# Reordered slots of an attention kernel beside its MLP: the norm's power behind the visit, stores and kept factors issued later

## The chip, the cores and the metric

The kernel runs on one core of a Trainium2 chip. The metric is the device time of one execution in microseconds (us); before the change the median of three runs is 1456.99 us. All data are float32. The engines are TensorE (PE, its weight loads are PEld), VectorE (DVE), ScalarE (ACT), GpSimd (POOL) and SyncE (SP), whose queue issues nearly all DMAs.

## The reference, cut to what matters

```python
def rmsnorm(x, g):
    rms = np.sqrt(np.mean(x * x, axis=-1, keepdims=True) + 1e-06)
    return x / rms * g
q_n, k_n = rmsnorm(q, g_q), rmsnorm(k, g_k)          # batch 8, heads 12, seq 448, head_dim 64
scores = np.matmul(q_n, k_n.transpose(0, 1, 3, 2)) / np.sqrt(64)
attn = np.exp(scores - scores.max(-1, keepdims=True))
attn = attn / (attn.sum(-1, keepdims=True) + 1e-09)
x = np.matmul(attn, v).transpose(0, 2, 1, 3).reshape(3584, 768)
h = x @ w_in                                         # 768 x 2048
out = (h - np.tanh(h)) @ w_out                       # 2048 x 768
```

## The kernel before, in words

Attention goes in 48 steps, one for each pair of heads of each batch (six to a batch). `slot(s)` does the values of step s and the scores of step s + 1, prepares the q and k of later steps, and lets the MLP of an earlier batch run between its pieces. The MLP is a generator (`mlp`): each `yield` tells the time of the matmul just written, and `run(ns)` draws matmuls until that much time is spent. Every engine works through its own queue in the order in which instructions are written, so the order of `slot`, `run` and the MLP is the order of all queues. There is no scheduler behind it.

**The visit.** `visit(s, av)` is PE's stretch of attention: scores of the last, short key chunk of step s + 1 (L552, exp into `p_last`), then values of step s in alternation with scores of chunks 0 and 1 (L618 and L552), the short chunk of values (L606), `divide`, and the scores of chunk 2. The score banks are three (`banks["sc"][:3]`), so the second wave of chunk 0 waits until the exp of `p_last` has emptied a bank. `divide` copies the values' sum (ACT L735), adds the other half (DVE L736) and multiplies by the reciprocal of the softmax sum (DVE L740, two).

**Between two visits** a slot has 14 points, with a fifteenth of its MLP time ahead of each and behind the last. In the kernel before they are, for steps in the block layout: scale q and k of step s + 2 by their norm (`scale_blocks`, L516); transpose q; transpose k (`turn_blocks`, L526, L530, then ACT L531) and load q/k of step s + 4 (`load_blocks`, L483, eight DMAs); the first addition of the softmax sum (L583) and the square of step s + 3 (ACT L487); the third chunk (L589); the norm's row sums (`norm_blocks`, L494); the short chunk (L596, two) and the exchange of the norm's halves (`meet_blocks`, ACT L501, four); transpose the softmax sum (`fold`, L693); its row sums (`fold_rest`, L700); half of `gather` (ACT L708, four) and `power_blocks`; the other half; `spread_sums` (DVE L716, L717, ACT L719); nothing; `turn_sums` (L725). `power_blocks` adds the halves (DVE L506), turns them into a mean (DVE L507) and has GpSimd raise it to the power -0.5 (POOL L509). The q/k tiles of step s + 4 take the place that step s + 2 leaves when L516 has read it (`qk_nat`, two buffers).

**The MLP.** Both layers are one level of Strassen's scheme with seven products in the order 1, 5, 6, 2, 3, 7, 4 (`ORDER`). A hidden layer (`hidden`, L804) has four groups of seven products; per group, a tanh on ACT and a subtraction that makes g (L850: product 2's on DVE, those of 3, 7 and 4 on POOL, written behind the product that follows, from `late["todo"]`). The tanh tile `th` has two buffers, and so have the others of `part`. Batch 0 is projected plainly (`project_first`, L1190), batch 1 by `project`; from batch 2 on two batches share a projection with two levels (`project_pair`, L1029), whose inner sums are POOL's (L1003, tile `u`, four buffers), apart from the four of its first outer product, which DVE makes at its start. Beside batch 1, `inner_steps` makes the inner factors of w_out on POOL (L955), one step a product, and keeps them in DRAM (`keep`, L937, five DMAs a factor), in a room that later holds `g2`.

**Weights** come through a ring of six slots (`ring_load`, L412 to L420): a product loads for the one four products later. Output tiles are transposed on DVE (L910) and stored with four DMAs (`store`, L913). Everything stands in SP's one queue: ring loads, q/k loads, v loads, kept factors, stores. In a slot beside a hidden layer its order is two v tiles, two ring loads, the eight q/k loads, five ring loads.

**Which MLP lies beside which slot** (`gap_ns`): slots 12 to 19 share batch 1's hidden layer, its projection and the first product of batch 2 evenly, 15.96 us each by the kernel's own count. Then, for each pair of batches, eight slots beside two hidden layers (15.7 us each) and four beside the projection (28.7 us each). The last pair has only four slots left.

## Time and profile before

| | |
|---|---|
| median of three runs | 1456.99 us (1453.01 to 1460.95) |
| the profiled execution | 1456.48 us, span 1454.7 us |
| mean granted clock of TensorE | 0.983 |
| busy: PE, DVE, POOL, ACT | 93%, 70%, 47%, 38% of the span |
| POOL's power, L509 | 33 times, 4843 ns each |
| POOL's inner sums, L1003 | 2217 to 2552 ns each |
| POOL's subtraction, L850 | 96 times, about 1.2 us each |
| w_f from w_in, w_inner, w_out | 4.0, 4.0, 4.6 us from issue to landing |
| slots 12 to 19 | 278.7 to 479.4 us |
| slots beside the hidden layers of two pairs | 479.4 to 674.9 and 826.0 to 1021.8 us |
| slots beside the first two `project_pair` | 674.9 to 826.0 and 1021.8 to 1173.1 us |
| slots 44 and 45 | 1173.1 to 1220.8 us |

How to read it: a slot is counted from the start of one visit (the L552 matmuls on 224 columns) to the start of the next. In the lists of waits a line is "engine line <- what ended the wait: total us, times, longest us". A line of the chain or of a timeline is "start us, duration us, engine, line, what". The windows give, for each stretch, the length, the busy time of PE, PEld, DVE, ACT and POOL with numbers of instructions, the granted clock, the DMA engines' busy share and GB/s. "issue" in the chain is time in which the engine waited for nothing that the profile shows; the long duration of a power on POOL appears in it.

### The profile page before, as it was taken

How to read it: one execution, taken by the hardware profiler on the slowest of the kernel's cores; microseconds unless marked ns; L12 is line 12 of the kernel's file. 1: busy time of each engine (PE TensorE's matmuls, PEld its weight loads, DVE VectorE, ACT ScalarE, POOL GpSimd, SP SyncE). 2: the span in 40 equal slices, each digit the busy share in tenths (PEclk: the TensorE clock that was granted, in tenths of full speed). 3: DMA queues.
4: the chain of work that ended last, by engine and by line, in shares of the span. 5: the costliest groups of instructions: out<-in, count | busy, mean ns of one | idle time of the engine just before them, and what ended most of it. 6: DMA issues, size and time to landing. Idle time of an engine off the chain costs nothing.

```text
span 1454.7 us, 29095 instructions
## 1 busy us (share of the span) xinstructions
PE 1352.1 (93%) x11336; PEld 1050.3 (72%) x11336; DVE 1012.3 (70%) x1471; ACT 552.9 (38%) x1326; POOL 685.2 (47%) x397
## 2 busy tenths in 40 slices
PE   7989899998799998999999999999989989999995
PEld 3468744576688787777766787878767678998884
DVE  5999898577786675668887775757988756323743
ACT  7856564334334444444222244453423233211000
POOL 4756474167653426243555534442645631423561
PEclk9999999999999999999999999999999999999998
DMA  7879787889787745464464764545536473555554
GB/s 171 193 200 293 229 233 197 233 256 309 261 230 229 185 115 175 105 184 113 128 161 113 180 193 114 144 144 136 170 103 173 116 192 110 163 174 156 147 144 99
DMA packets 371687, 253.53 MB, mean 174 GB/s; under 512 B 282196, under 2 KB 310228, under 8 KB 371540
## 3 DMA queue, kind: packets, MB, share of 16 engines
q1 hardware_dynamic: 371536, 251.57, 62.4%
q8 instruction: 92, 1.51, 0.4%
q14 instruction: 55, 0.45, 0.1%
q10 hardware_dynamic: 4, 0.00, 0.0%
HBM read 205.23 MB, written 46.27 MB: 173 GB/s over the span
## 4 chain that ended last, share of the span: by engine, by line
PE 36%; DVE 12%; issue 4%; POOL 1%; ACT 1%; DMA 1%; SPq 1%; DVEq 0%; POOLq 0%
PE mm L1029 17%; PE mm L804 12%; PE sc L552 4%; PE sc L618 2%; DVE rows L596 1%; DVE acc L1036 1%; DVE rows L589 1%; DVE rows L583 1%; DVE rr_mine L494 1%; DMA out_dram<-th 1%; DVE qk_n L516 1%; POOL rr_mine L509 1%; DVE qk_n L693 1%; DVE xT_more L740 1%; DVE s L1036 1%
## 5 line engine op out<-in xcount | busy, mean ns | idle before, releaser
L509 POOL TENSOR_TENSOR rr_mine<-rr_mine,neg_half 128x28 f32<-128x28 f32 x33 | 159.8, 4843 | 342.2 <-ACT sum_g L708 215.1
L552 PE MATMUL sc<-qT,kT 64*32 64x448 f32 (+1 forms) x3072 | 231.3, 513 | 37.1 <-ACT p_last L558 36.0
L804 PE MATMUL mm<-xT,w_f 128*128 128x224 f32 x1104 | 221.4, 354 | 9.3 <-DVE s L1036 4.1
L804 PE MATMUL mm<-tt,w_f 128*128 128x224 f32 x1044 | 211.7, 357 | 11.0 <-DMA w_f<-w_in 7.8
L804 PEld LDWEIGHTS mm<-xT,w_f 128*128 128x128 f32 x1104 | 207.4, 190 | 17.0 <-DVE s L1036 4.8
L804 PEld LDWEIGHTS mm<-tt,w_f 128*128 128x128 f32 x1044 | 197.3, 192 | 27.0 <-issue 13.6
L552 PEld LDWEIGHTS sc<-qT,kT 64*32 64x32 f32 x3072 | 76.9, 109 | 117.5 <-ACT p_last L558 52.8
L1029 PE MATMUL mm<-u,w_f 128*128 128x224 f32 x672 | 136.8, 354 | 8.9 <-issue 7.7
L1029 PEld LDWEIGHTS mm<-u,w_f 128*128 128x128 f32 x672 | 126.1, 190 | 13.9 <-issue 13.9
L618 PE MATMUL sc<-p,v_nat 64*32 64x448 f32 x1120 | 133.4, 566 | 0.0
L1029 PE MATMUL mm<-gT,w_f 128*128 128x224 f32 (+1 forms) x480 | 132.2, 429 | 0.7 <-DVE s L1036 0.7
L736 DVE TENSOR_TENSOR xT<-xT,sc 128x448 f32<-128x448 f32 x26 | 16.1, 621 | 163.4 <-PE sc L552 83.7
L1029 PEld LDWEIGHTS mm<-gT,w_f 128*128 128x128 f32 x480 | 90.4, 190 | 39.4 <-issue 37.1
L708 ACT COPY sum_g<-sum 32x14 f32<-32x14 f32 x280 | 56.3, 201 | 137.1 <-DVE sum L700 103.4
L1029 PE MATMUL mm<-g,w_f 128*128 128x224 f32 (+1 forms) x360 | 100.6, 434 | 4.7 <-DVE s L1036 4.7
L1029 PEld LDWEIGHTS mm<-g,w_f 128*128 128x128 f32 x360 | 68.4, 192 | 35.4 <-issue 29.1
L850 POOL TENSOR_TENSOR gT<-s,th 128x448 f32<-128x448 f32 x60 | 71.7, 1210 | 46.9 <-ACT th L849 44.7
L558 ACT ACTIVATE p<-sc 128x448 f32<-128x448 f32 x132 | 71.9, 545 | 45.9 <-PE sc L552 37.2
L849 ACT ACTIVATE th<-s 128x448 f32<-128x448 f32 x96 | 54.9, 575 | 68.2 <-POOL gT L850 21.4
L1190 PE MATMUL mm<-gT,w_out 128*128 128x448 f32 x192 | 74.6, 543 | 0.2 <-POOL w_out L90 0.2
L531 ACT ACTIVATE kT<-kT,g_col 128x448 f32<-128x448 f32 x33 | 22.1, 669 | 136.6 <-DVE kT L530 136.6
L1003 POOL TENSOR_TENSOR u<-g 128x896 f32<-128x896 f32 x18 | 39.9, 2217 | 68.0 <-PE mm L1029 40.8
(188 smaller groups left out, 2505.1 us busy)
## 6 DMA issues: line engine op xcount, KB each, us to landing
w_f<-w_in SPq DMA_DIRECT2D x196, 384.0 KB, 4.0
w_f<-w_inner SPq DMA_DIRECT2D x63, 512.0 KB, 4.0
w_f<-w_out SPq DMA_DIRECT2D x42, 512.0 KB, 4.6
w_raw<-in_moe_w_out_dram SPq DMA_DIRECT2D x16, 768.0 KB, 5.2
out_dram<-th SPq DMA_DIRECT2D x192, 56.0 KB, 2.0
w_in<-w_out SPq DMA_DIRECT2D x21, 384.0 KB, 5.2
qk_nat<-in_q_dram SPq DMA_DIRECT2D x132, 56.0 KB, 2.2
qk_nat<-in_k_dram SPq DMA_DIRECT2D x132, 56.0 KB, 2.3
```

The costliest lines, as they stand in the source:

```text
L509: nc.gpsimd.tensor_tensor(out=mine, in0=mine, in1=neg_half[:, :1].to_broadcast([P, 2 * NJ]), op=ALU.pow)
L552: nc.tensor.matmul(tiles[h][i * BL : (i + 1) * BL, :n], lhsT=kT[r, c * P + at : c * P + at + BL], rhs=qT[r, first : first + n], start=True ...
L558: nc.scalar.activation(p[:, h, c if c < 2 else 0, :], tiles[h][:, :n], AF.Exp, scale=1.0 if rr is None else rr[:, 0, 2 * c + h : 2 * c + h ...
L618: nc.tensor.matmul(av[g][i * BL : (i + 1) * BL, :S], lhsT=v_nat[keys, h, c, m * BL : (m + 1) * BL], rhs=p[keys, h], start=first, stop=True ...
L708: nc.scalar.copy(out=acc[h * BL : (h + 1) * BL, g], in_=part[g * BL : (g + 1) * BL, h * NJ : (h + 1) * NJ])
L804: nc.tensor.matmul(bank[:, f * HS : (f + 1) * HS], lhsT=w[:, c * width + f, :], rhs=moving[p](c), start=(first and f == 0 and c == 0), sto ...
L849: nc.scalar.activation(th, h, AF.Tanh, bias=0.0, scale=1.0)
L850: eng.tensor_tensor(out=g[:, rows, cols], in0=h, in1=th, op=ALU.subtract)
L1003: eng.tensor_tensor(out=u, in0=a, in1=z, op=ALU.subtract)
L1029: nc.tensor.matmul(bank[:, :n], lhsT=w(i), rhs=mv, start=(first and i == 0), stop=(i == len(moving) - 1), skip_group_check=not first,)
L1036: nc.vector.tensor_tensor(out=out, in0=x, in1=y, op=ALU.add)
L1190: nc.tensor.matmul(bank[:, :S], lhsT=w_out_row(f, n // HC)[:, n % HC * P : (n % HC + 1) * P], rhs=g[:, f, :], start=(f == 0), stop=(f == C ...
```

## The change

The power becomes a function of its own, and the slot's points are written in another order. The mean is finished late in the slot (`meet_rest`); the power itself is written directly behind the next visit, ahead of the first point. The additions of the softmax sum come first; scaling and transposing q and k follow, and `load_blocks` is written with the scaling. Squares, norm and exchange come behind `fold_rest`. `spread_sums` copies on DVE where it copied on ACT. Slots 12 to 14 lie beside the hidden layer of batch 1 (20.9 us of MLP each), slots 15 to 19 beside its projection and what is ahead (13.0 us each). A store's DMAs are written one product later, behind the next ring load (two steps later for batches 0 and 1); `step_out` counts. The kept inner factors are written one step later, in another order, and the next outer factor is fetched one step later. The four first inner sums of `project_pair` are now made on POOL during the odd batch's hidden layer, behind product 6 of each group (`first_inner`).

```diff
--- before.py
+++ after.py
@@ -500,12 +500,16 @@
         for g in range(P // BL):
             nc.scalar.copy(out=other[g * BL : (g + 1) * BL], in_=mine[(g ^ 1) * BL : ((g ^ 1) + 1) * BL])
 
-    def power_blocks(s):
+    def meet_rest(s):
 
         mine, other = normed["rr", s]
         nc.vector.tensor_tensor(out=mine, in0=mine, in1=other, op=ALU.add)
         nc.vector.tensor_scalar(out=mine, in0=mine, scalar1=1.0 / D, scalar2=1e-6, op0=ALU.mult, op1=ALU.add)
         normed["rr", s] = mine
+
+    def power_blocks(s):
+
+        mine = normed["rr", s]
         nc.gpsimd.tensor_tensor(
             out=mine, in0=mine, in1=neg_half[:, :1].to_broadcast([P, 2 * NJ]), op=ALU.pow
         )
@@ -716,7 +720,7 @@
         nc.vector.reduce_sum(total, acc.rearrange("p g j -> p j g"), axis=AX.X)
         nc.vector.reciprocal(total, total)
         wide = whole[s] = late["blocks"].tile([2 * BL, NJ, BL], F32, name="sum_w")
-        nc.scalar.copy(out=wide, in_=total[:, :, None].to_broadcast([2 * BL, NJ, BL]))
+        nc.vector.tensor_copy(out=wide, in_=total[:, :, None].to_broadcast([2 * BL, NJ, BL]))
 
     def turn_sums(s):
 
@@ -798,6 +802,7 @@
                 w = built(j, p).rearrange("p f (n d) -> p (f n) d", d=P)
             else:
                 ring_load(ring_steps.index((b, layer, j, p)) + 5)
+                step_out()
                 w = ring_tiles[b, layer, j, p].rearrange("p (n d) -> p n d", d=P)
             for f in range(width):
                 for c in range(depth):
@@ -863,6 +868,8 @@
 
             def use(p, bank):
                 v = view(bank)
+                if b > PAIRED and b % 2 and p == 6:
+                    first_inner(b - 1, j)
                 if j == SETS - 1 and p in ahead:
                     x_sums(b + 1, range(HC), ahead[p], nc.gpsimd)
                 if p == 1:
@@ -908,12 +915,22 @@
 
         o = part("th").rearrange("p f s -> p (f s)")
         nc.vector.transpose(out=o, in_=y if b >= FIRST else y.rearrange("r (c p) -> r p c", c=NCH))
-        for i in range(P // BL):
-            d = n * P + i * BL
-            nc.sync.dma_start(
-                out=out[b * S : (b + 1) * S, d : d + BL].rearrange("(j t) d -> t j d", t=BL),
-                in_=o[i * BL : (i + 1) * BL].rearrange("t (j d) -> t j d", d=BL),
-            )
+
+        def issue():
+            for i in range(P // BL):
+                d = n * P + i * BL
+                nc.sync.dma_start(
+                    out=out[b * S : (b + 1) * S, d : d + BL].rearrange("(j t) d -> t j d", t=BL),
+                    in_=o[i * BL : (i + 1) * BL].rearrange("t (j d) -> t j d", d=BL),
+                )
+
+        late["out"].append([1 if b >= PAIRED else 2, issue])
+
+    def step_out(by=1):
+        for entry in late["out"]:
+            entry[0] -= by
+        while late["out"] and late["out"][0][0] <= 0:
+            late["out"].pop(0)[1]()
 
     def calm_step(twice=False):
         for _ in range(1 + twice):
@@ -953,12 +970,13 @@
             )
             for n, (out, x, y, op) in enumerate(work):
                 yield lambda: nc.gpsimd.tensor_tensor(out=out, in0=x, in1=y, op=op)
-                if n == 0 and i + 1 < len(OUTER):
+                if n == 1 and i + 1 < len(OUTER):
                     fetch_outer(i + 1)
+            yield lambda: None
+            keep(i, 1, block(sums, 0, 2))
+            keep(i, 4, block(sums, 2, 2))
             keep(i, 0, a11)
-            keep(i, 1, block(sums, 0, 2))
             keep(i, 3, a12)
-            keep(i, 4, block(sums, 2, 2))
             keep(i, 6, a22)
             yield lambda: None
 
@@ -970,6 +988,15 @@
             else:
                 fn()
 
+    def first_inner(b, i):
+
+        g, us = late["g", b], late.setdefault("us", {})
+        KB = HF // 2
+        x11, x12, x21, x22 = (g[:, f : f + KB, cols] for f in (0, KB) for cols in (slice(0, HS), slice(HS, S)))
+        u = us[1, i] = late["pair"].tile([P, KB, HS], F32, name="u", bufs=4)
+        a, z = ((x12, x11), (x22, us.get((1, 0))), (x22, x12), (x21, us.get((1, 1))))[i]
+        nc.gpsimd.tensor_tensor(out=u, in0=a, in1=z, op=ALU.subtract)
+
     def project_pair(b):
 
         g = [late.pop(("g", b)), late.pop(("g", b + 1))]
@@ -977,7 +1004,7 @@
         KB = HF // 2
         HOME = {1: (0, 0), 5: (0, 0), 3: (1, 1), 6: (1, 1), 2: (0, 1), 4: (0, 1), 7: (1, 0)}
         acc, acc2 = (late["pair"].tile([P, HC, S], F32, name=name) for name in ("acc", "acc2"))
-        us = {}
+        us = late.pop("us")
 
         def rows(p, f, n, cols):
             which, half = HOME[p]
@@ -1011,9 +1038,6 @@
         }
         inner_plan = {5: 0, 6: 1, 7: 2, 4: 3}
         inner_at = {6: 0, 3: 1, 7: 2, 4: 3}
-        for i in range(4):
-            inner_sum(OUTER[0], i, V)
-
         def at(k, q):
 
             p = OUTER[k]
@@ -1078,6 +1102,7 @@
         for k, p in enumerate(OUTER):
             step = ring_steps.index((b, 2, p, 0))
             ring_load(step + 5)
+            step_out()
             w = ring_tiles[b, 2, p, 0].rearrange("p (f d) -> p f d", d=P)
             bank = mm_bank()
             q = 0
@@ -1093,6 +1118,7 @@
             banks = {}
             for i, q in enumerate(ORDER):
                 ring_load(step + 6 + i // 2)
+                step_out()
                 w = ring_tiles[b, 2, p, 1 + i // 2][:, i % 2 * HB : (i % 2 + 1) * HB].rearrange("p (f d) -> p f d", d=P)
                 first = q not in (2, 3, 7)
                 bank = banks[q] = mm_bank() if first else banks[{2: 1, 3: 5, 7: 6}[q]]
@@ -1172,6 +1198,8 @@
             n = (k + HC) % CD
             if f == 0:
                 bank = mm_bank()
+            if f == CF // 2:
+                step_out(2)
             if k < HC:
                 weight(CF + HF + HF * (m + 1) // (HC * CF))
             elif m < HC * CF + 2:
@@ -1203,7 +1231,7 @@
         late["inner"] = inner_steps()
 
     def mlp():
-        late["todo"], late["keep"], late["inner"], late["calm"] = [], [], None, []
+        late["todo"], late["keep"], late["inner"], late["calm"], late["out"] = [], [], None, [], []
         for b in range(PAIRED):
             yield from hidden(b)
             yield from project(b) if b else project_first(b)
@@ -1222,6 +1250,8 @@
             fn()
         while late["calm"]:
             calm_step()
+            step_out()
+        step_out(2)
 
     stream = mlp()
     spent = [0.0, 0.0]
@@ -1244,8 +1274,10 @@
 
         if s < 2 * NP:
             return H_NS / 12 if s % NP < 3 else 4 * S / ENGINE_NS * CD * CF / 12
+        if s < 2 * NP + 3:
+            return H_NS / 12
         if s < 2 * NP + 8:
-            return (H_NS + O_NS + AHEAD_NS) / 32
+            return (O_NS + AHEAD_NS) / 20
         return (H_NS if (s - 2 * NP - 8) % 12 < 8 else PAIR_NS) / 16
 
     def has(s):
@@ -1339,30 +1371,25 @@
         folded = following and s + 1 >= FOLDED
         first = s + 3 == TURNED
 
-        def scale_or_turn():
-            if first:
-                turn(s + 2, sc_bank(), sc_bank())
-            else:
-                scale_blocks(s + 2)
-
+        scaled = rows and not first
+        normed_now = ahead and not first
+        if scaled:
+            power_blocks(s + 2)
         work = (
-            ((rows, scale_or_turn),),
-            ((rows and not first, lambda: turn_blocks(s + 2, 0)), (first, lambda: load_blocks(s + 3))),
-            ((rows and not first, lambda: turn_blocks(s + 2, 1)), (has(s + 4), lambda: load_blocks(s + 4))),
-            ((following, lambda: add(s + 1, False)), (ahead and not first, lambda: square_blocks(s + 3))),
-            ((following, lambda: add_third(s + 1)),),
-            ((ahead and not first, lambda: norm_blocks(s + 3)),),
-            ((following, lambda: add_last(s + 1)), (ahead and not first, lambda: meet_blocks(s + 3))),
+            ((following, lambda: add(s + 1, False)), (first, lambda: turn(s + 2, sc_bank(), sc_bank()))),
+            ((following, lambda: add_third(s + 1)), (first, lambda: load_blocks(s + 3))),
+            ((following, lambda: add_last(s + 1)),),
+            ((scaled, lambda: scale_blocks(s + 2)), (has(s + 4), lambda: load_blocks(s + 4))),
+            ((scaled, lambda: turn_blocks(s + 2, 0)),),
+            ((scaled, lambda: turn_blocks(s + 2, 1)),),
             ((folded, lambda: fold(s + 1)),),
-            ((folded, lambda: fold_rest(s + 1)), (first, lambda: square_blocks(s + 3))),
-            (
-                (folded, lambda: gather(s + 1, 0)), (ahead and not first, lambda: power_blocks(s + 3)),
-                (first, lambda: norm_blocks(s + 3)),
-            ),
-            ((folded, lambda: gather(s + 1, 1)), (first, lambda: meet_blocks(s + 3))),
-            ((folded, lambda: spread_sums(s + 1)), (first, lambda: power_blocks(s + 3))),
+            ((folded, lambda: fold_rest(s + 1)), (ahead, lambda: square_blocks(s + 3))),
+            ((folded, lambda: gather(s + 1, 0)),),
+            ((ahead, lambda: norm_blocks(s + 3)), (folded, lambda: gather(s + 1, 1))),
+            ((ahead, lambda: meet_blocks(s + 3)), (folded, lambda: spread_sums(s + 1))),
             (),
-            ((folded, lambda: turn_sums(s + 1)),),
+            ((folded, lambda: turn_sums(s + 1)), (ahead, lambda: meet_rest(s + 3))),
+            (),
         )
         for point in work:
             run(4 * gap / (len(work) + 1))
```

## The prediction

> **What bounds the kernel now.** I read the page, the waits of TensorE (PE), the chain in order of time, the timelines of single engines, then SP's waits. PE is busy 93% of the span, so only what makes it wait or run slower counts.
>
> The waits of PE (total, times, longest) name ScalarE's exp of the last key chunk. The windows below them show an unstalled slot, a stalled one, and a stretch at half clock:
>
> ```profile
> PE sc L552 <- ACT p_last L558: 36.0, 18, 4.9
> PE mm L804 <- DMA w_f<-w_in: 7.8, 2, 5.8
> ```
>
> And the windows (us of the window; busy us and instructions of PE, PEld, DVE, ACT, POOL; granted clock; DMA):
>
> ```profile
> 479.40:500.90 21.50, 21.50 (x213) 18.17 (x212) 14.71 (x25) 9.80 (x26) 7.31 (x5) 1.00 0.87 225
> 526.80:551.10 24.30, 22.50 (x216) 18.95 (x215) 15.52 (x26) 11.15 (x30) 8.10 (x5) 1.00 0.50 142
> 506.60:510.00 3.40, 3.40 (x56) 2.18 (x47) 0.00 (x0) 1.63 (x3) 0.00 (x0) 0.50 0.00 0
> ```
>
> A slot (one visit of attention, then a quarter of a hidden layer) takes 21.5 us unstalled, about 24.25 us stalled: 2.75 us lost in each of 15 slots (7 beside each of the first two pairs of batches, one beside the third). Each of four stretches like the last line costs a further 1.7 us there. Who causes the stall is in the chain:
>
> ```profile
> 648.04 1.10 POOL rr_mine L509
> 649.14 3.65 issue
> 652.79 1.14 POOL g L850
> ...
> 653.95 0.58 ACT th L849
> 654.52 0.42 ACT s L869
> 654.94 0.27 ACT p_last L558
> ...
> 655.25 0.56 PE sc L552
> ```
>
> GpSimd's power (L509) starts 2.6 us before the visit of 650.63 and runs 4.78 us. The subtraction at L850 queues behind it, a tanh needs the buffer that L850 frees, and `p_last` stands behind that tanh on ScalarE. PE waits until 655.25.
>
> The wait that is hidden today is on SP: first its longest wait of all, then its timeline and PE's in the slot that ends with this visit:
>
> ```profile
> SPq L483 <- DVE qk_n L516: 246.7, 26, 15.9
> ```
>
> ```profile
> 637.82 1.90 SPq L483 DMA_DIRECT2D qk_nat<-in_q_dram  x4
> 639.76 2.04 SPq L483 DMA_DIRECT2D qk_nat<-in_k_dram  x4
> 641.90 4.61 SPq L412 DMA_DIRECT2D w_f<-w_in  x5
> ```
>
> ```profile
> 648.27 2.43 PE L804 MATMUL mm<-xT,w_f 128*128 128x224 f32 x12
> ```
>
> SP stands at the q/k loads until `scale_blocks` (L516) ends; five ring loads queue behind. The first holds the weights of product 1, the last before the next visit. It is issued at 641.90, takes 3.7 us to land (the view of `w_f`; the five reach 4.9), and PE wants it at 648.27: 2.7 us to spare.
>
> **What the Trainium skill says.** *DMA: Bandwidth & Descriptors*, "Anatomy of one DMA — SWDGE (gpsimd) path": a DMA's semaphore wait happens on the issuing sequencer. The SP lines agree: 246.7 us of waiting, with later loads behind. *SBUF — State Buffer*, "SBUF: two separate sides": a VectorE instruction with two SBUF inputs and a GpSimd one exclude each other, each for its whole length. It agrees for GpSimd's subtractions: L583 takes 1.08 us alone and 2.76 beside one (687.76). It does not for the power: L996 takes 1.08 us inside one (704.37). *TensorE: Matmul & The Clock Gate*, "Part 1: The HAM clock gate (the "warmup" mystery)": after idling, the clock is halved for about 3.4 us. The 0.50 line agrees. No page prices the power; the trace does.
>
> **The change, part by part.** Times are after V, the start of L736 behind a visit (634.68 here); PE wants product 1 at V+13.6.
>
> *Power behind the visit.* POOL's queue becomes subtraction, power, subtraction. The power's input comes from `meet_rest`, last on VectorE before the visit. So it runs about V-3.5 to V+1.3, in the visit, where POOL has nothing else to do. `p_last` then waits only for VectorE: laid out with the trace's durations it starts 1.8 us earlier than today, leaving some 0.9 us of the 2.75. By itself: 15 x 1.85 = 28 us gained, up to 41 with the whole stall, plus up to 5 x 1.7 of half clock.
>
> *Order of the slot.* `add`, `add_third` and `add_last` now precede the scaling. L516 ended at V+3.1. From the starts of the trace: L736 0.65, two L740 1.34, L583 1.18, L871 0.53, L589 1.01, two L596 1.30, L873 0.54, L516 1.09, sum V+7.6. The loads at L483 keep their place in SP's order: two ring loads, eight q/k loads, five ring loads. So the eight start at V+7.7 and take 4.1 us, the load for product 1 goes out at V+11.8 and lands at V+15.5. PE waits 1.9 to 2.0 us in every slot that has q/k loads. Bounds: 1.0 if the rest of the order saves VectorE a microsecond, 3.2 with the slowest landing. ScalarE catches up in that time, so the two stalls don't add; the new one replaces the old: 7.6 (L516) + 4.2 (q/k) + 3.7 (landing) + 2.4 (product) + 5.5 (unstalled visit with its restart) + 0.1 = about 23.5, say 23.6 us a slot, against 24.25.
>
> *First inner sums on POOL.* Four subtractions of 1.07 to 2.04 us leave VectorE at the head of `project_pair`, where PE has no idle time today: nothing gained. In the odd batch's hidden layer POOL gets one of 2.2 us (L1003: 2239 ns) per slot. Nothing holds it back, so it starts when the power ends, V+1.3, amid L740, L583 and L589, all with two SBUF inputs: one of them waits about 2.2 us. L516, SP and product 1 follow: 25.8 us for the slots of odd batches. Bounds: 0 if it falls between them, 2.2.
>
> Sum for the two stretches beside hidden layers (479.4 to 674.9, 826.0 to 1021.8; 391.3 us now): 8 x 23.6 + 8 x 25.8 = 395.2, plus half clock after idle stretches of 2 to 4 us, taken at six (four today, four to ten possible): 10.2. That is 405.4, or 14 more. Beside the third pair nothing is left to load, so there the stall and its half clock go: -4.6.
>
> *3 and 5 slots in batch 1* (278.7 to 479.4, 200.7 us). The MLP share is 20.9 and 13.0 us instead of 15.96. Four slots beside the hidden layer lose about 22 us today, 11 of them before a `w_f` load that came late behind q/k loads and kept factors (PE mm L804, 5.8, then half clock). In the three new ones POOL runs its sums of 1.27 us straight after the power, against VectorE's adds: L516 at V+11 to 12, ring loads behind the q/k loads 4 to 7 us late in two slots, with half clock about 17 in all. In the five short ones VectorE's 16 us of work and ScalarE's copies for the norm (`meet_blocks`, now close to the visit) run some 3.5 us into it, so `p_last` is late by about 2 each: 10, where 1 is lost now. Together +4; bounds -15 and +12.
>
> *Stores and kept factors later.* The stores stand behind one ring load more; the five kept DMAs a step later no longer wait for POOL (1 to 4 us a time). Worth up to -5 (in the span of batch 1, inside its bounds); a store's `th` buffer comes free at most one product later. Zero, covered by the other `th` buffer; without it L910 waits, as 18.2 us in all do now.
>
> *The spread copy on VectorE.* 0.56 us off ScalarE (L719), on VectorE 0.25 to 0.65; no row shows it, I take 0.5, ahead of nothing that PE waits for. Zero.
>
> *Slots beside `project_pair`* (302.4 us, some 27 lost to VectorE and the bank): the adds move ahead of PE's bank copies, four sums leave. Zero, bounds -8 and +8.
>
> **Sum:** 14 - 4.6 + 4 = 13.5. The profiled execution took 1456.5 (span 1454.7 and 1.8 around it; the median of the runs is 1457.0), so 1470.
>
> **Rivals.** (1) Faster: the load is not what ends the wait, because SP gets to it in time. It decides below about V+9.7 for the issue. Then even slots take 22.4 and odd ones 24 (0.9 us and 2.2 us of port left): 371 instead of 391, -5 in the third pair, -12 in batch 1, since the late `w_f` there goes too: 1419. For it: stalls named by the page are all ScalarE's and POOL's; against it: SP's queue order and eight issues of half a microsecond. (2) Nothing in the sum: the inner sum meets no VectorE instruction, batch 1 breaks even, and the adds ahead of the bank copies cost 8 beside `project_pair`. Then 16 x 23.6 + 7 = 385 (-6), -4.6 and +8: about 1454. For it: the port is only held 2.2 us a slot; against it: three of VectorE's four first instructions need it. (3) Slower still: every stall of an odd slot brings half clock and `project_pair` takes its upper bound: 1486.
>
> **Numbers.** Forecast (1462 to 1482) 0.43; rival 1 (1405 to 1445) 0.30; rival 2 (1446 to 1464) 0.15; rival 3 (1482 to 1495) 0.12. The range must reach into rival 1: 1418 to 1487. Half a per cent, 7 us, is about what a measurement can tell from no change: faster 0.31, same 0.16, slower 0.53. The likeliest case alone: 1462 to 1482.
>
> **What would show it.** Right: PE sc L552 <- ACT p_last near zero, and in its place waits of product 1 (L804) for DMA w_f<-w_in, some 2 us, 16 times; SP's wait at L483 ending about V+7.7; slots of 23.6 and 25.8 us, VectorE's longer where POOL subtracts behind the power. Wrong: unstalled slots of 21.5 to 22 us (rival 1), `p_last` still late in them, or the loss sitting in batch 1 or `project_pair`.

## The result and the profile after

The changed kernel takes 1456.66 us (median of 12 runs, 1451.67 to 1458.57), the kernel before in the same measurement 1460.43 us (1453.01 to 1462.06). The ratio is 0.9977, 95% interval 0.9963 to 0.9991: 3.4 us faster, inside the half per cent, where 1470 had been forecast. The profiled execution took 1454.87 us, span 1453.1, against 1454.7 before, so the two traces are compared stage by stage. First what PE waits for in the changed kernel:

```profile
PE mm L809 <- DMA w_f<-w_in: 22.1, 10, 5.2
PE mm L809 <- DVE s L884: 10.6, 5, 2.3
PE sc L556 <- ACT p_last L562: 10.2, 6, 5.2
```

The wait for `p_last`, 36.0 us in 18 cases before, is down to 10.2 us, none of it beside a hidden layer of batches 2 to 5. In its place stands `w_f`, 7.8 us before. The second line is the same wait under another name: a matmul that waits for several semaphores is put down to the one that came last by the profile, and run 7 below, which moves only loads, removes both lines.

Then the windows of six stages: slots 12 to 19, the hidden layers of the first pair, its `project_pair`, the same two of the second pair, slots 44 and 45. Of the kernel before:

```profile
278.67:479.41 200.74, 184.45 (x1726) 151.95 (x1725) 147.66 (x204) 84.23 (x227) 112.12 (x65) 0.98 0.82 248
479.41:674.87 195.46, 182.02 (x1692) 151.17 (x1691) 124.01 (x200) 87.78 (x230) 73.71 (x45) 0.98 0.55 152
674.87:826.00 151.13, 142.72 (x1024) 105.60 (x1023) 122.64 (x164) 41.85 (x115) 91.12 (x44) 0.99 0.53 135
826.00:1021.82 195.82, 182.27 (x1692) 151.16 (x1691) 126.21 (x206) 87.69 (x230) 69.03 (x41) 0.98 0.55 152
1021.82:1173.13 151.31, 141.30 (x1023) 104.95 (x1022) 122.71 (x165) 41.72 (x115) 90.70 (x44) 1.00 0.54 136
1173.13:1220.82 47.69, 45.57 (x425) 37.68 (x424) 31.28 (x52) 20.10 (x52) 9.19 (x5) 0.96 0.56 160
```

And of the changed kernel:

```profile
277.93:469.04 191.11, 182.83 (x1726) 152.92 (x1725) 141.59 (x204) 78.47 (x210) 108.28 (x67) 0.99 0.83 255
469.04:669.88 200.84, 181.61 (x1691) 147.92 (x1690) 150.35 (x215) 86.83 (x233) 82.29 (x47) 0.97 0.52 148
669.88:821.48 151.60, 143.29 (x1024) 107.08 (x1023) 119.53 (x169) 38.62 (x109) 88.01 (x43) 0.98 0.54 140
821.48:1021.20 199.72, 179.15 (x1691) 145.09 (x1690) 148.29 (x209) 85.26 (x223) 80.48 (x47) 0.98 0.51 147
1021.20:1174.71 153.51, 143.98 (x1023) 107.83 (x1022) 119.22 (x167) 38.63 (x109) 88.32 (x42) 0.98 0.54 138
1174.71:1219.73 45.02, 44.19 (x426) 37.03 (x425) 32.58 (x50) 18.98 (x50) 10.81 (x6) 1.00 0.59 165
```

The first number behind the two ends of a window is the stage's length: -9.6 in batch 1, +9.3 in the two hidden stretches together, +2.7 beside the paired projections, -2.7 in slots 44 and 45; the rest of the span gives -1.3. The forecast had +4, +14, 0 and -4.6. So two large movements cancel, and the one with the wrong sign is batch 1.

The hidden stretches move as forecast, by less. SP, POOL, VectorE and PE in one odd-batch slot of the changed kernel (V, the start of L740, which was L736 before, is 623.79 here):

```profile
633.26 1.90 SPq L483 DMA_DIRECT2D qk_nat<-in_q_dram  x4
635.20 2.04 SPq L483 DMA_DIRECT2D qk_nat<-in_k_dram  x4
637.34 2.32 SPq L412 DMA_DIRECT2D w_f<-w_in  x5
```

```profile
620.28 4.78 POOL L513 TENSOR_TENSOR rr_mine<-rr_mine,neg_half 128x28 f32<-128x28 f32 x1
625.03 2.08 POOL L998 TENSOR_TENSOR u<-gT 128x896 f32<-128x896 f32 x1
```

```profile
623.79 0.62 DVE L740 TENSOR_TENSOR xT<-xT,sc 128x448 f32<-128x448 f32 x1 [3.60 <-ACT xT L739]
624.45 3.13 DVE L744 TENSOR_TENSOR xT<-xT,rs_T 64x448 f32<-64x448 f32 x2
627.61 1.09 DVE L587 TENSOR_TENSOR rows<-p 128x896 f32<-128x896 f32 x1
628.62 0.62 DVE L878 TENSOR_TENSOR s<-mm,s 128x448 f32<-128x448 f32 x1
629.16 1.08 DVE L593 TENSOR_TENSOR rows<-rows,p_full 128x896 f32<-128x896 f32 x1
630.27 1.27 DVE L600 TENSOR_TENSOR rows<-rows,p_last 64x448 f32<-64x448 f32 x2
631.57 0.62 DVE L880 TENSOR_TENSOR s<-mm,s 128x448 f32<-128x448 f32 x1
632.12 1.08 DVE L520 TENSOR_TENSOR qk_n<-qk_nat,rr_mine 128x896 f32<-128x896 f32 x1
```

```profile
636.25 2.54 PE L809 MATMUL mm<-tt,w_f 128*128 128x224 f32 x12 [0.99 <-DVE g L855]
640.81 0.43 PE L809 MATMUL mm<-xT,w_f 128*128 128x224 f32 x1 [2.02 <-DMA w_f<-w_in]
```

The power now ends inside the visit. The scaling (L520) ends at V+9.4, because `u` runs across the two multiplications by the reciprocal at L744: 3.13 us for the pair, where run 4, without `u`, shows 1.27. The q/k loads start 0.06 us after the scaling, the ring load for product 1 goes out at V+13.6, and PE stands still for 2.02 us until it lands.

### The profile page after: what moved, and what is told of

Its sections match the earlier page's. It is cut to its first block, busy times and chain, and to the rows that moved or that the text cites. A ratio compares the mean times of both kernels' runs of the same rounds, so it can differ in the third digit from the quotient of the medians.

```text
span 1453.1 us, 29070 instructions
## 1 busy us (share of the span) xinstructions
PE 1348.9 (93%) x11336; PEld 1045.7 (72%) x11336; DVE 1044.5 (72%) x1494; ACT 535.4 (37%) x1291; POOL 705.5 (49%) x409
## 3 DMA queue, kind: packets, MB, share of 16 engines
q8 instruction: 92, 1.51, 0.4%
## 5 line engine op out<-in xcount | busy, mean ns | idle before, releaser
L809 PE MATMUL mm<-xT,w_f 128*128 128x224 f32 x1104 | 231.0, 365 | 36.3 <-DMA w_f<-w_in 16.9
L809 PEld LDWEIGHTS mm<-xT,w_f 128*128 128x128 f32 x1104 | 214.1, 196 | 47.1 <-DVE s L884 19.8
L556 PE MATMUL sc<-qT,kT 64*32 64x448 f32 (+1 forms) x3072 | 219.5, 505 | 11.5 <-ACT p_last L562 10.2
L1053 PEld LDWEIGHTS mm<-u,w_f 128*128 128x128 f32 x672 | 127.5, 192 | 16.2 <-issue 15.7
L556 PEld LDWEIGHTS sc<-qT,kT 64*32 64x32 f32 x3072 | 72.0, 107 | 85.3 <-issue 52.2
L855 POOL TENSOR_TENSOR g<-s,th 128x448 f32<-128x448 f32 x36 | 41.0, 1141 | 162.6 <-ACT th L854 162.6
L622 PE MATMUL sc<-p,v_nat 64*32 64x448 f32 x1120 | 115.7, 536 | 0.0
L740 DVE TENSOR_TENSOR xT<-xT,sc 128x448 f32<-128x448 f32 x26 | 16.2, 621 | 115.5 <-PE sc L556 69.2
L1030 POOL TENSOR_TENSOR u<-gT 128x896 f32<-128x896 f32 x18 | 40.4, 2246 | 69.0 <-PE mm L1053 69.0
```

The source lines that it names most:

```text
L556: nc.tensor.matmul(tiles[h][i * BL : (i + 1) * BL, :n], lhsT=kT[r, c * P + at : c * P + at + BL], rhs=qT[r, first : first + n], start=True ...
L622: nc.tensor.matmul(av[g][i * BL : (i + 1) * BL, :S], lhsT=v_nat[keys, h, c, m * BL : (m + 1) * BL], rhs=p[keys, h], start=first, stop=True ...
L740: nc.vector.tensor_tensor(out=x, in0=x, in1=av[1][:, :S], op=ALU.add)
L809: nc.tensor.matmul(bank[:, f * HS : (f + 1) * HS], lhsT=w[:, c * width + f, :], rhs=moving[p](c), start=(first and f == 0 and c == 0), sto ...
L855: eng.tensor_tensor(out=g[:, rows, cols], in0=h, in1=th, op=ALU.subtract)
L1030: eng.tensor_tensor(out=u, in0=a, in1=z, op=ALU.subtract)
```

## The experiments

All times are medians; each ratio is against runs of the kernel before on the same chip (1459.6 to 1460.4 us), with its 95% interval. Where a gain over the kernel before is given in us, it is worked out from that ratio. Stage lengths are from one profile of each kernel. How far one such number can be trusted: the changed kernel and run 4 have the same code in batch 1 and show 191.1 and 194.5 us there, and the stretch ahead of slot 12 shows 262.1 to 270.0 us over all these profiles, also where no edit reaches it.

**1. The changed kernel with eight equal slots in batch 1.**

```diff
-        if s < 2 * NP + 3:
-            return H_NS / 12
         if s < 2 * NP + 8:
-            return (O_NS + AHEAD_NS) / 20
+            return (H_NS + O_NS + AHEAD_NS) / 32
```

> The changed kernel with eight equal slots beside batch 1 again. Theory 1 (the split into 3 and 5 slots is what won 9.6 us of the span there): the loss returns, slots 12 to 19 take about 200 us instead of 191, the time is about 1466. Theory 2 (the later stores and kept factors won it, by taking SP out of the way of ring loads): slots 12 to 19 stay at 191 to 194, the time within 2 us of 1457.

Measured: 1470.11 us, 1.0056 (1.0038 to 1.0075); slots 12 to 19 take 203.4 us. The split matters, as theory 1 says; the time is 4 us longer than it expected.

**2. The changed kernel with stores and kept factors issued as before.** (`store` issues its four DMAs at once; `keep` and `fetch_outer` stand where the kernel before has them.)

> The changed kernel with stores and kept factors issued where the kernel before issues them. Theory 1 (split): slots 12 to 19 stay within 3 us of 191, the time is 1457 to 1460. Theory 2 (later issue): slots 12 to 19 go back to about 200, the time is about 1466.

Measured: 1471.34 us, 1.0080 (1.0059 to 1.0101); slots 12 to 19 take 201.9 us. So theory 2 is right as well, and neither is right alone: in the changed kernel, undoing either loses the whole gain of batch 1. This was not expected, and runs 5, 6, 10, 13 and 14 take it up from the kernel before.

**3. The scaling ahead of the additions again, everywhere.**

```diff
         work = (
-            ((following, lambda: add(s + 1, False)), (first, lambda: turn(...))),
-            ((following, lambda: add_third(s + 1)), (first, lambda: load_blocks(s + 3))),
-            ((following, lambda: add_last(s + 1)),),
-            ((scaled, lambda: scale_blocks(s + 2)), (has(s + 4), lambda: load_blocks(s + 4))),
-            ((scaled, lambda: turn_blocks(s + 2, 0)),),
-            ((scaled, lambda: turn_blocks(s + 2, 1)),),
+            ((scaled, lambda: scale_blocks(s + 2)), (first, lambda: turn(...))),
+            ((scaled, lambda: turn_blocks(s + 2, 0)), (first, lambda: load_blocks(s + 3))),
+            ((scaled, lambda: turn_blocks(s + 2, 1)), (has(s + 4), lambda: load_blocks(s + 4))),
+            ((following, lambda: add(s + 1, False)),),
+            ((following, lambda: add_third(s + 1)),),
+            ((following, lambda: add_last(s + 1)),),
```

> The changed kernel, with the scaling and the two turns of q and k ahead of the three additions, as in the kernel before; the power stays behind the visit, so the q/k loads can go out some 4 us earlier. Load theory (the place of the scaling is what makes product 1's weights late): PE's waits before product 1 go, the slots beside hidden layers take about 22 us for even batches and 23 to 24 for odd ones, 30 to 36 us less in the sum: about 1424. Rival (VectorE's work is late whatever its order: the additions, now later, hold up the visit): the stalls come back at p_last and the time stays at 1450 to 1458.

Measured: 1437.24 us, 0.9848 (0.9824 to 0.9873). The hidden stretches give 31.9 us (368.7 in place of 400.6; 22.2 us a slot in even batches, 23.9 in odd ones), as the load theory says. The total was missed by 13 us: batch 1 is 8.6 us longer (199.7) and the paired projections 5.8 us. There the new order looks like the better one, by one profile of each kernel.

**4. The first inner sums back on VectorE.** (`first_inner` is not called; the four `inner_sum(OUTER[0], i, V)` stand at the head of `project_pair` again.)

> The changed kernel with the four first inner sums back on VectorE at the head of the paired projection. Port theory (GpSimd's 2.1 us subtraction keeps VectorE's instruction, and so the loads behind the scaling, waiting): the eight slots of odd batches fall from a mean of 25.7 us to the 24.4 of the even ones, 11 us less: about 1446. Rival (the sums meet no wait that PE feels, or what is won is paid back at the head of the paired projection by four instructions of 1 to 2 us): 1455 to 1459.

Measured: 1443.30 us, 0.9888 (0.9868 to 0.9908), 13 us below the changed kernel. The odd batches' slots fall from 25.7 to 24.0 us, and the paired projections stay the same (304.2 us, 305.1 with the sums on GpSimd). VectorE behind a visit in this run:

```profile
601.11 1.27 DVE L744 TENSOR_TENSOR xT<-xT,rs_T 64x448 f32<-64x448 f32 x2
...
606.89 1.08 DVE L520 TENSOR_TENSOR qk_n<-qk_nat,rr_mine 128x896 f32<-128x896 f32 x1
```

V is 600.45, so the scaling ends at V+7.5, as it does in all eight slots of the odd batches in this run. The port theory holds: moving the sums to GpSimd cost 13 us, since GpSimd keeps VectorE waiting and SP and PE stand behind VectorE.

**5 and 6. The kernel before with the split alone, and with the split and the later issue.** (The edits of runs 1 and 2 in the other direction.)

> The kernel before with only the split into 3 and 5 slots beside batch 1. If the split wins by itself, slots 12 to 19 fall from 200.7 us to 190 to 194 and the time is about 1451. If it wins only together with the later issue (with either of the two undone in the changed kernel, 202 to 203 us stood in place of 191), slots 12 to 19 stay at 199 to 206 and the time is 1459 to 1466.

> The kernel before with the split and the later stores and kept factors; the power, its place and VectorE's order stay as they were. If these two together are the gain in batch 1: slots 12 to 19 at 190 to 194 us, the hidden stretches unchanged at 391, about 1451. If the order of VectorE's work (additions first) is needed too, as the 199.7 us of the run with the scaling first suggest: slots 12 to 19 at 198 to 201, 1457 to 1460.

Measured: split alone 1457.22 us, 0.9982 (0.9970 to 0.9995), slots 12 to 19 at 195.5 us; with the later issue 1451.35 us, 0.9939 (0.9921 to 0.9957), 187.6 us. The two together are the whole gain of batch 1, without the power's move and without the new order. The split alone landed between its two cases; with the later issue slots 12 to 19 came out 2.4 us shorter than expected.

**7. The changed kernel with the q/k loads at the end of the slot's work.**

```diff
-            ((scaled, lambda: scale_blocks(s + 2)), (has(s + 4), lambda: load_blocks(s + 4))),
+            ((scaled, lambda: scale_blocks(s + 2)),),
...
             ((folded, lambda: turn_sums(s + 1)), (ahead, lambda: meet_rest(s + 3))),
-            (),
+            ((has(s + 4), lambda: load_blocks(s + 4)),),
```

> The changed kernel with the q/k loads written at the end of the slot's work, behind the slot's ring loads; VectorE's order stays (additions first). Load theory: product 1's weights no longer stand behind the eight q/k loads, PE's waits before product 1 go although the scaling is as late as before; slots beside hidden layers about 22 us (even batches) and 23 to 24 (odd), the time about 1425. Rival (it is VectorE's late work itself that PE waits for, through banks or the layer's own additions): slots stay at 24.4 and 25.7 and the time within 6 us of 1457.

Measured: 1431.56 us, 0.9804 (0.9791 to 0.9817). VectorE is as late as in the changed kernel, and yet PE no longer waits for `w_f` from `w_in` at all. What PE waits for most is now:

```profile
PE sc L556 <- ACT p_last L562: 19.6, 18, 4.8
PE mm L1053 <- issue: 9.9, 7, 2.2
```

So it was the load that PE stood waiting for. But the load is not the whole price of the late scaling. The windows of batch 1 and of the two hidden stretches in this run:

```profile
278.21:461.81 183.60, 180.99 (x1725) 151.64 (x1724) 142.58 (x204) 78.47 (x210) 110.04 (x67) 1.00 0.88 270
461.81:653.19 191.38, 182.22 (x1691) 149.48 (x1690) 150.33 (x210) 83.92 (x228) 80.68 (x45) 1.00 0.59 154
803.95:997.26 193.31, 183.22 (x1692) 149.49 (x1691) 147.42 (x205) 82.25 (x218) 79.35 (x45) 0.99 0.60 156
```

Of the 25 us that came back, 7.5 are in batch 1 and only 15.9 beside the hidden layers, where the scaling first (run 3) gave 31.9. A slot of an even batch takes 24.4 us in the changed kernel, 23.4 here and 22.2 in run 3. In 14 of the 16 slots PE now waits 0.5 to 1.7 us for `p_last`. So about half of the loss there is the load and the other half is not; that this half is VectorE's lateness by another way, through `p_last`, fits the waits and run 3, but no run takes it apart.

**8. The scaling first in the slots beside hidden layers only, and the first inner sums on VectorE.** (`scales` and `adds` are the two halves of run 3's list, the q/k loads at the second turn.)

```diff
+        beside_hidden = s >= 2 * NP + 8 and (s - 2 * NP - 8) % 12 < 8
+        work = (scales + adds if beside_hidden else adds + scales) + (
```

> The changed kernel with the scaling first in the slots beside hidden layers of batches 2 to 5 alone, and the first inner sums on VectorE. If the two costs add (late q/k loads, and the port in odd batches): all sixteen slots at 22 to 22.5 us, 355 us in place of 400.6, the rest as in the changed kernel: 1411 to 1416. If they overlap (the sum on VectorE alone already gave 8.1 and 5.5 back in the odd batches, the scaling first 7.2 and 7.1), odd slots stay at 23.5 or more: 1420 or more.

Measured: 1407.44 us, 0.9631 (0.9612 to 0.9649): the fastest kernel of this study, 3.7% below the kernel before. The two costs add, within 3 us (357.8 us of hidden stretches, 355 expected). Its hidden stretches, 179.9 and 177.9 us:

```profile
464.99:644.91 179.92, 177.52 (x1691) 149.26 (x1690) 143.16 (x213) 85.97 (x233) 73.34 (x42) 1.00 0.60 167
795.79:973.71 177.92, 176.14 (x1691) 148.02 (x1690) 141.70 (x208) 84.44 (x223) 72.05 (x42) 1.00 0.61 168
```

PE is busy 98.8% of these two stretches together, at full clock in both. The same queue of SP, and PE at product 1 (V is 607.04):

```profile
610.20 1.90 SPq L483 DMA_DIRECT2D qk_nat<-in_q_dram  x4
612.14 2.04 SPq L483 DMA_DIRECT2D qk_nat<-in_k_dram  x4
614.28 4.58 SPq L412 DMA_DIRECT2D w_f<-w_in  x5
```

```profile
620.63 1.68 PE L809 MATMUL mm<-xT,w_f 128*128 128x224 f32 x8
```

The ring load goes out at V+7.2 and product 1 starts at V+13.6 without a wait.

**9. The kernel before with only the power behind the visit.**

```diff
-    (folded, lambda: gather(s + 1, 0)), (ahead and not first, lambda: power_blocks(s + 3)),
+    (folded, lambda: gather(s + 1, 0)), (ahead and not first, lambda: meet_rest(s + 3)),
...
+        if rows and not first:
+            power_blocks(s + 2)
```

> The kernel before with only GpSimd's power moved behind the visit (its mean and the rest of the norm stay where they were; scaling, turns and q/k loads keep their places). The step of the forecast for the power by itself says 28 us gained, up to 41 with the half clock; the run with the scaling first and the sums on VectorE gave 33.5 us in the sixteen slots: 1424 to 1430. If the power holds something else up in the place of the subtraction, under 15 us gained: over 1445.

Measured: 1424.53 us, 0.9750 (0.9736 to 0.9763): 36.5 us gained by this one edit. The hidden stretches take 355.4 us, as short as in run 8:

```profile
483.19:660.71 177.52, 176.05 (x1691) 147.06 (x1690) 123.17 (x200) 86.47 (x229) 71.04 (x42) 1.00 0.59 167
814.03:991.86 177.83, 175.94 (x1692) 146.89 (x1691) 125.62 (x206) 86.58 (x229) 68.25 (x41) 1.00 0.60 167
```

**10. The kernel before with only the later issue.**

> The kernel before with only the later stores and kept factors. The two edits in batch 1 together gave 9 us, the split alone 3. If they add: 6 us gained, about 1454, slots 12 to 19 at 194 to 196 us. If the later issue pays only with the split: no gain, 1459 to 1462.

Measured: 1455.06 us, 0.9958 (0.9943 to 0.9973), slots 12 to 19 at 194.8 us. On the kernel before, the two parts add within their intervals: -2.6 us for the split, -6.1 for the later issue, -8.9 for both.

**11. The spread copy back on ScalarE.** (L723 is `nc.scalar.copy` again.)

> The changed kernel with the spread copy back on ScalarE. On VectorE it takes 1.08 us in the trace of the changed kernel, where the forecast had 0.5 and priced it at nothing. If that is right: 1455 to 1458. If the copy (1.08 us ahead of the turn of the sums and of the norm's mean) makes the scaling and so the loads later in each slot: up to 1 us in each of 16 slots, 1441 to 1448.

Measured: 1457.74 us, 0.9985 (0.9974 to 0.9996), the changed kernel's time. What the copy is worth can't be told from nothing, though on VectorE it takes 1.08 us and not 0.5.

**12. Run 8 with the q/k loads at the end of the slot outside the hidden layers.**

> The fastest kernel so far (scaling first beside hidden layers, first sums on VectorE; 1407.4) with the q/k loads at the end of the slot in all other slots. If the load also sets what is left in batch 1 (183.6 us with late loads, 187.6 here): 1402 to 1405. If the 4 us are only the scatter of that stretch (187.6 to 194.5 in three kernels with the same code there): 1406 to 1410.

Measured: 1408.11 us, 0.9641 (0.9626 to 0.9656), the same time as run 8. Batch 1 does show 183.8 us as in run 7, but slots 32 to 35, right behind the first paired projection, take 92.5 us in place of 87.8. In these two profiles the gain is given back there; run 12's profile is of the slowest of its five executions (1411.04 us). The expectation named scatter as the reason for no gain, and said that three kernels have the same code in batch 1; that holds for two of them, since run 8 writes the q/k loads two points later in these slots too.

**13 and 14. The later issue taken apart on the kernel before: kept factors alone, stores alone.**

> The kernel before with only the kept factors (and the fetches of their sources) issued a step later; stores as before. If the kept factors are the gain of 5 us of the later issue (SP's wait of 13.5 us at L937 for GpSimd goes, and ring loads behind it come earlier): 1454 to 1456, slots 12 to 19 at 195 to 197 us. If not: 1459 to 1462.

> The kernel before with only the stores issued later; kept factors as before. If the stores are the gain (SP waits 88.6 us at L913 for VectorE's turn, with ring loads behind): 1454 to 1456. If the kept factors are: 1459 to 1462, slots 12 to 15 as before at 113 us together.

Measured: kept factors 1455.66 us, 0.9970 (0.9959 to 0.9982), 4.4 us gained (2.6 to 6.0); stores 1458.52 us, 0.9993 (0.9978 to 1.0008), not to be told from nothing, with slots 12 to 15 at 111.2 us together. The kept factors are most of it. SP in the kernel before, ahead of the 5.8 us for which PE waited there:

```profile
371.99 1.90 SPq L483 DMA_DIRECT2D qk_nat<-in_q_dram  x4
373.94 2.05 SPq L483 DMA_DIRECT2D qk_nat<-in_k_dram  x4
376.03 3.56 SPq L937 DMA_DIRECT2D w_inner<-g  x5
379.69 1.08 SPq L412 DMA_DIRECT2D w_f<-w_in  x1
```

And in the run with the kept factors later, at the same place of the slot:

```profile
377.20 1.90 SPq L483 DMA_DIRECT2D qk_nat<-in_q_dram  x4
379.15 2.04 SPq L483 DMA_DIRECT2D qk_nat<-in_k_dram  x4
381.29 0.42 SPq L412 DMA_DIRECT2D w_f<-w_in  x1
381.75 0.90 SPq L930 DMA_DIRECT2D g<-w_out  x2
382.75 1.43 SPq L420 DMA_DIRECT2D w_f<-w_out  x3
384.27 3.86 SPq L937 DMA_DIRECT2D w_inner<-g  x5
```

The five issues that stood between the q/k loads and the ring load now stand behind it. PE's longest wait for `w_f` falls from 5.8 us to 2.6 in that run. Slots 12 to 19 were missed: 197.9 us measured with the kept factors, 195 to 197 expected.

## Why the prediction was wrong, point by point

The step that failed is batch 1. The forecast took the new split as a loss of 4 us and put the later issue of stores and kept factors at nothing; slots 12 to 19 became 9.6 us shorter in the changed kernel, and on the kernel before the two edits gain 2.6 and 6.1 us. The steps beside the hidden layers, power, order and sums, were right in kind.

**The power behind the visit: right, and undersized.** The forecast was "28 us gained, up to 41 with the whole stall, plus up to 5 x 1.7 of half clock". Run 9 gives 36.5 us (34.6 to 38.5). The remainder of 0.9 us a slot that was kept back for VectorE did not show in the even batches (21.8 us a slot) and only in part in the odd ones (22.6, 0.4 us idle).

**The order of the slot: right, and undersized.** L516 at V+7.6 was forecast; in five of the eight slots of even batches the scaling ends at V+7.5 (V+8.7 at most), the q/k loads start at once, and PE is idle 2.05 us a slot on the mean, against 1.9 to 2.0 forecast. Such a slot takes 24.4 us (24.1 without half clock), where 23.6 had been forecast. That PE waits for the load is shown by run 7, that the order causes it by runs 3 and 8. What the forecast left out is a second cost of the order, which run 7 shows: moving the loads away gives back 1.0 us of an even slot, moving the scaling 2.2. This is rival 1 refuted: SP reaches the ring load at V+11.7 to V+13.6, not before V+9.7.

**First inner sums on POOL: right in mechanism, oversized.** 2.2 us a slot were forecast. The scaling ends at V+8.5 to V+9.5 in the odd batches, 0.9 to 2.0 us later, PE's idle time is 2.85 us a slot, and the slots take 25.7 us on the mean, half clock included, where the forecast had 25.8 without it. Without half clock they take 24.9. Undone, 13 us come back (run 4). The term for VectorE and GpSimd excluding each other, for which the forecast named the Trainium skill's *SBUF — State Buffer*, "SBUF: two separate sides", agrees with the trace: 3.13 us in place of 1.27 at L744.

The two hidden stretches were to rise by 14 us and rose by 9.3: the difference is 3 us in the slots and 1.7 us in half clock (five stretches and not six).

**Slots 44 and 45:** -4.6 forecast, -2.7 measured: the stall there is down to 0.8 us, not to zero. **Beside the paired projections:** 0 forecast, +2.7 measured, inside the bounds. **Spread copy:** nothing forecast, nothing measured.

**3 and 5 slots in batch 1: wrong, and with the kept factors the cause of the wrong sign.** The forecast was "about 17 in all" lost in the three new slots and "about 2 each: 10" in the five short ones, against 22 and 1 lost before: "Together +4". The scaling in the three was forecast at V+11 to 12. It ends at V+10.1 in slot 13 and at V+9.4 in slot 14; slot 12 has none, since step 14 is not yet in the block layout. Of two late ring loads one came, in slot 13:

```profile
334.76 1.46 PE L809 MATMUL mm<-tt,w_f 128*128 128x224 f32 x3 [5.16 <-DMA w_f<-w_in]
```

PE's idle time is 0.5, 5.2 and 0.3 us in the three, with one half-clock stretch (1.7 us) 7.7 us in all. In the five short ones PE is idle 2.2 us in all, not 10: `p_last` is late by 1.2 us in slot 16 and 1.0 in slot 19, and not at all in the other three. VectorE has 14.4 to 16.7 us of work in these slots, as forecast, but they last 18.9 to 21.0 us. That is 9.9 us lost where 27 were forecast. Counted the same way the kernel before lost 19.6 (16.2 idle and 3.4 of half clock), not 23. The difference, 9.7, is the 9.6 by which the stage is shorter, counted a second time in the same two traces; it says where the time went, not which edit did it. Runs 5, 6 and 10 say that: slots 12 to 19 take 195.5 us with the split alone, 194.8 with the later issue alone, and 187.6 with both, where the kernel before takes 200.7.

**Stores and kept factors later: wrong.** The forecast said "Worth up to -5" and put nothing into the sum. Run 10 shows -6.1 us by itself on the kernel before, and run 13 about -4.4 of it for the kept factors. The forecast had the cause in hand: its paragraph on batch 1 names a `w_f` load "that came late behind q/k loads and kept factors", with 11 us lost before it. But it priced the move of the kept factors only by their wait for POOL, and not by that ring load, which now goes out ahead of them.

The sum of forecast less measured by stages: 13.6 in batch 1, 4.7 in the hidden stretches, -1.9 in slots 44 and 45, -2.7 beside the pairs, 1.3 elsewhere: 15, the gap between 13.5 forecast and -1.6 in the two spans. Batch 1 is nine tenths of it. Rival 2 named nearly the measured time (1454), but that was luck: it had the inner sum meet no VectorE instruction and batch 1 break even, and both are refuted. Rival 3 is refuted too: four of the eight stalls in odd batches brought half clock, and the paired projections lost 2.7 us and not 8.

So where the large gain went: the power's 36.5 us and batch 1's 8.9 us add up to 45, and the kernel gained 3.4. The other 42 were given back by the same change, by the scaling behind the additions (36 us between runs 4 and 8, which differ in that beside hidden layers, and by two points in the place of the q/k loads elsewhere) and by the sums on GpSimd (13 us, run 4). These two come to 49 and not to 42: the change without them, run 8, gains 54 and not 45, and that difference is open (below).

**What stays open.** Split and later issue are worth 2.6 and 6.1 us on the kernel before, but about 12 and 15 us on the changed one, where the scaling is late (runs 1 and 2 against the changed kernel, by their ratios). That SP's queue has less slack there is an argument, not a measurement; in the profiles slots 12 to 19 are 12.3 and 10.8 us longer than in the changed kernel, 5.1 and 6.8 of it by half clock. Run 8 is 8.5 us better than run 9 and run 6 taken together. In the profiles 5.0 us of it lie in the stretch ahead of slot 12 of run 9, which that edit doesn't touch, and 7 us beside the paired projections; no run tells why.

## What to carry to other kernels

Before work is put behind other work on an engine, follow what waits for it one queue further: here VectorE's scaling freed buffers, SP stood at loads into these buffers, and the weights that PE needed stood behind those loads. When a change gains by one part and loses by another, make each part alone; one part of this change was worth ten times the whole. Write an in-order DMA queue by when its results are needed, not by when its sources are ready: that gave 25 us in run 7 and 4.4 in run 13, though nothing in run 12.

## What the runs showed of the hardware that was not expected

Two VectorE multiplications of 64x448 take 1.27 us alone and 3.13 beside GpSimd's subtraction of 2.08 us, while a VectorE subtraction of 128x896 (L996 of the kernel before, at 704.37) took 1.08 us in the middle of GpSimd's power. That power took 5.49 us, 4.84 on the mean. So it is not enough that GpSimd is at work; whether the kind of its operation or its small size (128x28) makes the difference, no run tells.

Sixteen stalls of PE beside hidden layers in the changed kernel last 1.3 to 3.2 us, and five of them were followed by 3.4 us at half clock, at 539.4, 590.6, 641.8, 966.1 and 993.4 us. These starts lie whole multiples of 3.413 us apart (51.2 is 15 of them, 27.3 is 8). When the trace is cut into steps on that beat, each of the five stalls leaves PE idle for 2.02 us or more in one step, and none of the other eleven for more than 1.9. The longest of all brought no half clock:

```profile
1018.78 0.61 PE L1053 MATMUL mm<-gT,w_f 128*128 128x448 f32 x1 [3.15 <-DVE sum_all L721]
```

The beat at 1017.27 cuts it into 1.64 and 1.51 us, while the 2.02 us ahead of 640.81 fell into one step. Over all sixteen traces, from slot 12 to slot 45, more than 2.01 us of idle time in a step at full clock was always followed by half clock, less than 1.70 never, and between the two both happened. So a count of half-clock stretches, as the forecast's six, can't be had from the length of the stalls alone.
